# Six fixed PSUM banks in the attention, and one mask-and-maximum step for four of them

## The chip, the core and the metric

The kernel runs on one core of a Trainium2 chip. The metric is the device time of one execution in microseconds (us). A core has engines that run side by side and in order, each from its own instruction queue: TensorE (PE, with its weight loads shown as PEld), VectorE (DVE), ScalarE (ACT), GpSimd (POOL) and SyncE (SP, which issues most DMAs here). They are tied together by semaphores: an instruction may wait until another engine's counter has reached a value. PE writes its results into PSUM, which has eight banks of 512 fp32 columns; DVE and ACT read them from there.

## The reference

One transformer block with a parallel sum: the layer norm of x feeds both an attention with a sliding window and a gated feed-forward part, and both are added to x.

```python
S, D, H, W = 2048, 640, 32, 256; Dh = 20; Df = 1728
xn = layernorm(x)
q, k, v = split(xn @ wqkv)                       # 32 heads of 20 columns
scores = einsum("bhqd,bhkd->bhqk", q, k) * Dh ** -0.5
mask = (idx[:, None] - idx[None, :] >= 0) & (idx[:, None] - idx[None, :] < W)
p = softmax(where(mask, scores, -1e9))
attn = einsum("bhqk,bhkd->bhqd", p, v) @ wo
ffn = (gelu(xn @ w_gate) * (xn @ w_up)) @ w_down
out = x + attn + ffn
```

## The kernel before, in words

The program has four stretches: layer norm and the first projections (to about 107 us), the attention with other matmuls mixed in (to about 570 us), the rest of the feed-forward's gate and up matmuls (to about 804 us), and the output matmuls.

The attention works through 32 units: 8 groups of 4 heads times 4 chunks of 512 queries. A unit u needs three kinds of PE work, all of them written by one hand-made order of slots (`attention()`, line 805; 14 slots per unit, `NS`), which PE, DVE, ACT, POOL and SP follow as written:

- **Maxima.** The softmax's row maxima are computed first, from a bfloat16 product. `max_pair(u, i)` (line 503) fills two banks (`ps_m`) with 128 rows by up to 288 keys, by 16 or more small matmuls (L523) that sit side by side in the array, and DVE then adds the mask and takes the maximum in one instruction per bank (L527), which the profile shows as two rows, CUSTOM_DVE_ANT_0 and DVE_READ_ACCUMULATOR2_ANT. Two pairs make a *burst* of four banks; `BURSTS` puts one at slots 0, 4 and 8, and in slot 0 a second one follows the `av` step below. Twelve slots ahead of unit 0 do seven bursts in advance. A unit has four bursts, which belong to a later unit. After the last one, `max_end` transposes the maxima through PE (`ps_n`, L544), ACT copies them out (`mr`, L546), and a DMA puts them into the rows of q so that the score matmul subtracts them.
- **Scores.** `exp_piece(u, s)` (line 568) fills one bank (`ps_e`, L582, one or two matmuls, 512 columns in all) and ACT takes the exponential into SBUF (`P`, L584). A unit has twelve pieces; `SCORES` says which stand in which slot: 1, 4, 2, 2 and 3 of them in slots 0, 2, 4, 8 and 10. POOL clears the masked corners (L595, L598).
- **The value product.** `av_unit(u - 1)` (line 601) multiplies `P` with v into one bank (`ps_o`, L609) in slot 0, between its two bursts, and ACT copies it out (`ob`, L613).

Between them each slot runs RATE / NS = 2.43 steps of *filler*: dense matmuls of the projections and of the feed-forward part (`ps_d` and `ps_v`, L110), whose two banks come from another pool (`psd`). Small DVE and ACT steps of these projections are put behind the slot's own work by `late` and `flush`.

All the attention's banks come from one pool of six:

```python
psr = pp.enter_context(tc.tile_pool(name="psr", bufs=6, space=PSUM, reuse_waits="tile"))
def bank(name):
    return psr.tile([128, C], F32, name=name, tag="ring")
```

Each call of `bank` gives a new tile in the next of six buffers, and the first instruction that writes it waits for whoever read that buffer's last tile. These waits are put in when the program is built.

Of the kernel before, what the change touches and what calls it, by code (L numbers as in the profile page):

```python
# [9 lines left out]
F32 = mybir.dt.float32  # L10
# [9 lines left out]
C = 512  # L20
# [12 lines left out]
SCORES = {0: range(0, 1), 2: range(1, 5), 4: range(5, 7), 8: range(7, 9), 10: range(9, 12)}  # L33
# [37 lines left out]
def block_kernel(ctx, tc, x, wqk, wv, wgu, wdo, wdl, out):  # L71
# [58 lines left out]
    mask = st1.tile([128, 288], F32, name="mask")  # L130
# [293 lines left out]
    with tc.tile_pool(name="lp", bufs=1, side="right") as lp:  # L424
# [21 lines left out]
        for c in range(1, NC):  # L446
            ln_scale(xs[4 * c:4 * c + 4], lp, mv1 if c == 1 else None)
            vs = [proj_v(v0, 4 * c - 4 + i, None if i % 2 else (psm, "mx")) for i in range(4)]
            if c == 1:
                with tc.manual_schedule(engines={mybir.EngineType.PE}):  # L450
                    lead = (cost for gen in vs for cost in gen)
                    for _ in range(VLEAD):
                        next(lead)
                    ln_turn(4 * c, xs[4 * c:4 * c + 4])
                    run(lead)
            else:
                ln_turn(4 * c, xs[4 * c:4 * c + 4])
            if c + 1 < NC:
                xs += [ln_load(t, lp) for t in range(4 * c + 4, 4 * c + 8)]
            if c == 1:  # L460
                for i in range(NQ):
                    for j in (0, 2):
                        nc.sync.dma_start(qs[i][SR + 2:64, j:j + 2].rearrange("p j t -> p (j t)"), ones[2:4])
            if c == 2:
                for z in range(4):
                    band = mask if z == 0 else lp.tile([128, D], F32, name="xi", tag="xi", bufs=8)[:, 0:288]
                    nc.gpsimd.memset(band, 0.0)
                    nc.gpsimd.affine_select(out=band, in_=band, pattern=[[1, 288]], compare_op=OP.is_ge,
                                            fill=NEG, base=32 * z - 1, channel_multiplier=-1)
                    nc.gpsimd.affine_select(out=band, in_=band, pattern=[[-1, 288]], compare_op=OP.is_ge,  # L470
                                            fill=NEG, base=256 - 32 * z, channel_multiplier=1)
# [26 lines left out]
    def bank(name):  # L498
        return psr.tile([128, C], F32, name=name, tag="ring")

    maxes = {}

    def max_pair(u, i):
        g, c = divmod(u, NC)
        jj, b = divmod(i, 4)
# [3 lines left out]
        n = 128 * b + 128 if c == 0 and b < 2 else 288  # L509
        pss = [bank("ps_m") for _ in range(2)]  # L510
        todo = []
        for h in range(4):
            q0 = 128 * b + 32 * h
            k0 = q0 + 32 - n
            parts = [(max(0, -k0), n, k, max(0, k0), q0 + 32)]
            if k0 < 0:
                parts.append((0, -k0, ks[(u - 1) % NK], C + k0, C) if c else (0, -k0, k, 0, None))
            todo += [(i_, h, q0, *part) for i_, part in enumerate(sorted(parts, key=lambda p: p[1] - p[0]))]
        for _, h, q0, lo, hi, kt, k0, k1 in sorted(todo, key=lambda p: p[:2]):
            for r, ps in enumerate(pss):  # L520
                rows, j = slice(64 * r, 64 * r + SR), 2 * r + jj
                keys = kt[rows, j, k0:k1] if k1 else kt[rows, j, 0:1].to_broadcast([SR, hi])
                nc.tensor.matmul(ps[32 * h:32 * h + 32, lo:hi], q[rows, j, q0:q0 + 32], keys,  # L523
                                 start=True, stop=True, tile_position=(64 * r, 32 * h))
        junk = ap.tile([128, 288], BF, name="junk", tag="junk", bufs=1)
        for r, ps in enumerate(pss):
            nc.vector.tensor_tensor_reduce(out=junk[:, 0:n], in0=ps[:, 0:n], in1=mask[:, 288 - n:288], scale=1.0,  # L527
                                           scalar=NEG, op0=OP.add, op1=OP.max,
                                           accum_out=maxes[u][:, 2 * r + jj, b:b + 1])
# [11 lines left out]
    def max_end(u):  # L541
        nm = maxes.pop(u)
        ps = bank("ps_n")
# [24 lines left out]
    def exp_piece(u, s):  # L568
# [9 lines left out]
        ps = bank("ps_e")  # L578
# [22 lines left out]
    def av_unit(u):  # L601
        g, c = divmod(u, NC)
        o, v = bank("ps_o"), vtiles[g]
# [179 lines left out]
    stream = ((u, i) for u in range(NU) for i in range(8))  # L783
# [3 lines left out]
    def pull_max(n, slot):  # L787
        for _ in range(n):
# [3 lines left out]
            max_pair(*x)  # L792
            if x[1] == 7:
# [11 lines left out]
    def attention():  # L805
# [18 lines left out]
        for u in range(NU + 1):  # L824
            for i in range(NS):
# [9 lines left out]
                for s in SCORES.get(i, ()) if u < NU else ():  # L835
                    exp_piece(u, s)
# [672 lines left out]
```

## Time and profile before

| | before |
|---|---|
| time, median of 3 runs (lowest to highest) | 1046.93 us (1046.66 to 1049.24) |
| the profiled execution: own time, span of its trace | 1046.71 us, 1045.0 us |
| busy: PE, DVE, ACT, POOL | 1034.0, 717.1, 513.6, 335.9 us |
| attention, 107.5 to 553 us of the span: PE, DVE, ACT, POOL busy | 441.90, 271.55, 278.41, 264.72 us of 445.5 |
| maxima on DVE (L527, 512 banks) | 227.9 us, and 42.6 us for the accumulator reads |

A span runs from the first to the last instruction; the profiled execution's own time is 1.7 us more. Busy time counts the time in which at least one instruction of the engine is open; PE's matmuls overlap each other, so a row of PE is longer than the time that it keeps the next one away. "idle before" in a row is the idle time of the engine just ahead of it, with an arrow to the instruction that ended it. The chain of waits follows the work that ended last back from the end: it gives each stretch to the engine that held it.

### The profile page before, as it was taken

How to read it: one execution, taken by the hardware profiler on the slowest of the kernel's cores; microseconds unless marked ns; L12 is line 12 of the kernel's file. 1: busy time of each engine (PE TensorE's matmuls, PEld its weight loads, DVE VectorE, ACT ScalarE, POOL GpSimd, SP SyncE). 2: the span in 40 equal slices, each digit the busy share in tenths (PEclk: the TensorE clock that was granted, in tenths of full speed). 3: DMA queues.
4: the chain of work that ended last, by engine and by line, in shares of the span. 5: the costliest groups of instructions: out<-in, count | busy, mean ns of one | idle time of the engine just before them, and what ended most of it. 6: DMA issues, size and time to landing. Idle time of an engine off the chain costs nothing.

```text
span 1045.0 us, 25814 instructions
## 1 busy us (share of the span) xinstructions
PE 1034.0 (99%) x9533; PEld 826.2 (79%) x9533; DVE 717.1 (69%) x2007; ACT 513.6 (49%) x1088; POOL 335.9 (32%) x511
## 2 busy tenths in 40 slices
PE   8999999999999999999999999999999999999998
PEld 8987666666677766666667888888888999999998
DVE  8745656666655556666663678877656888888887
ACT  4444666765665666555656522223324553333332
POOL 5222767766464458464634111110110000000000
PEclk9999999999999999999999999999999999999999
DMA  5552465545332355444322556677217864443342
GB/s 200 189 150 61 136 185 157 174 152 183 98 117 74 106 148 153 129 131 140 103 80 82 191 193 235 220 254 246 100 61 255 272 232 137 136 128 114 124 136 92
DMA packets 105192, 158.76 MB, mean 152 GB/s; under 512 B 15421, under 2 KB 60093, under 8 KB 105065
## 3 DMA queue, kind: packets, MB, share of 16 engines
q1 hardware_dynamic: 102680, 150.95, 45.1%
q10 hardware_dynamic: 2384, 6.16, 1.8%
q8 instruction: 75, 1.23, 0.5%
q14 instruction: 53, 0.43, 0.1%
HBM read 101.78 MB, written 54.92 MB: 150 GB/s over the span
## 4 chain that ended last, share of the span: by engine, by line
PE 89%; DVE 3%; DMA 3%; POOL 2%; SPq 1%; ACT 1%; issue 1%; DVEq 0%; POOLq 0%
PE ps_g L953 21%; PE ps L1220 21%; PE ps_d L110 19%; PE ps_e L582 7%; PE ps_v L110 7%; PE ps_o L609 7%; PE ps_m L523 4%; PE ps_g L110 1%; DMA qs<-qd 1%; SPq L494 1%; PE ps_t L181 1%; DMA qd<-pt 1%; POOL pt L259 1%; PE ps_d L356 1%; POOL wql L643 0%
## 5 line engine op out<-in xcount | busy, mean ns | idle before, releaser
L527 DVE CUSTOM_DVE_ANT_0 junk<-ps_m,mask 128x288 bf16<-128x288 f32 (+2 forms) x512 | 227.9, 445 | 155.0 <-PE ps_m L523 97.2
L584 ACT ACTIVATE P<-ps_e 128x512 f32<-128x512 f32 (+2 forms) x384 | 195.6, 578 | 59.8 <-PE ps_e L582 56.1
L1220 PE MATMUL ps<-wb,at 128*128 128x320 f32 x999 | 155.9, 309 | 0.0
L1220 PEld LDWEIGHTS ps<-wb,at 128*128 128x128 f32 x999 | 148.9, 188 | 0.2
L595 POOL TENSOR_SCALAR_AFFINE_SELECT P<-P 128x512 f32<-128x512 f32 x128 | 84.6, 663 | 139.1 <-ACT P L584 138.1
L582 PE MATMUL ps_e<-qs,ks 124*128 124x128 bf16 (+2 forms) x704 | 107.4, 277 | 0.6 <-DVE mx L527 0.5
L110 PE MATMUL ps_d<-xh,wqh 128*128 128x512 f32 x350 | 104.3, 410 | 0.0
L110 PE MATMUL ps_d<-xl,wqh 128*128 128x512 f32 x350 | 104.3, 409 | 0.0
L110 PE MATMUL ps_d<-xh,wql 128*128 128x512 f32 x350 | 103.9, 409 | 0.0
L1220 PE MATMUL ps<-wt,at 128*128 128x320 f32 x552 | 89.3, 309 | 0.4 <-DVE u L1058 0.4
L582 PEld LDWEIGHTS <-ks 124*128 124x128 bf16 x704 | 50.9, 98 | 46.5 <-issue 29.0
L609 PE MATMUL ps_o<-P,v 128*32 128x384 f32 (+2 forms) x1408 | 84.9, 386 | 0.7 <-POOL P L598 0.7
L1220 PEld LDWEIGHTS ps<-wt,at 128*128 128x128 f32 x552 | 82.9, 188 | 0.9 <-DVE u L1058 0.9
L598 POOL TENSOR_SCALAR_AFFINE_SELECT P<-P 128x512 f32<-128x512 f32 x112 | 70.3, 638 | 33.6 <-ACT P L584 33.6
L1174 ACT ACTIVATE at<-ss 128x512 fp32r<-128x512 f32 x59 | 37.3, 632 | 87.6 <-DVE ss L1058 87.5
L103 POOL TENSOR_TENSOR wql<-wr,wqh 128x640 fp32r<-128x640 f32 x11 | 17.6, 1607 | 174.8 <-PE ps_g L953 149.5
L609 PEld LDWEIGHTS ps_o<-P,v 128*32 128x32 f32 x1408 | 41.0, 109 | 40.5 <-issue 20.4
L110 PEld LDWEIGHTS ps_d<-xh,wql 128*128 128x128 f32 x350 | 63.9, 189 | 11.1 <-issue 0.4
L110 PEld LDWEIGHTS ps_d<-xl,wqh 128*128 128x128 f32 x350 | 63.8, 189 | 10.4 <-issue 0.2
L110 PEld LDWEIGHTS ps_d<-xh,wqh 128*128 128x128 f32 x350 | 63.5, 189 | 10.7 <-issue 0.2
L259 POOL TENSOR_TENSOR pt<-r,pt 128x512 bf16<-128x512 f32 x40 | 46.8, 1169 | 63.2 <-ACT pt L258 63.0
L613 ACT ACTIVATE ob<-ps_o 128x512 f32<-128x512 f32 x32 | 19.1, 598 | 86.3 <-PE ps_o L609 76.1
(194 smaller groups left out, 1846.8 us busy)
## 6 DMA issues: line engine op xcount, KB each, us to landing
hr<-hd SPq DMA_DIRECT2D x104, 128.0 KB
hd<-he SPq DMA_DIRECT2D x50, 256.0 KB
wr<-wgu SPq DMA_DIRECT2D x27, 320.0 KB
qs<-qd SPq DMA_DIRECT2D x64, 120.0 KB
ks<-kd SPq DMA_DIRECT2D x64, 120.0 KB
xi<-x SPq DMA_DIRECT2D x16, 320.0 KB
qs<-qd SPq DMA_DIRECT2D x64, 80.0 KB
ks<-kd SPq DMA_DIRECT2D x64, 80.0 KB
```

The lines of the kernel that those rows point to most:

```text
L110: nc.tensor.matmul(ps, a(k), b(k), start=n == 0, stop=n == 3 * nk - 1)
L259: nc.gpsimd.tensor_tensor(out=pt[:, l, :], in0=r, in1=pt[:, 1, :], op=OP.subtract)
L523: nc.tensor.matmul(ps[32 * h:32 * h + 32, lo:hi], q[rows, j, q0:q0 + 32], keys, start=True, stop=True, tile_position=(64 * r, 32 * h))
L527: nc.vector.tensor_tensor_reduce(out=junk[:, 0:n], in0=ps[:, 0:n], in1=mask[:, 288 - n:288], scale=1.0, scalar=NEG, op0=OP.add, op1=OP.max ...
L582: nc.tensor.matmul(ps[:, col:col + n], k[0:QROWS, j, kc:kc + 128], q[0:QROWS, j, q0:q0 + n], start=True, stop=True)
L584: nc.scalar.activation(pt[:, j, lo:hi], ps[:, lo:hi], AF.Exp, scale=SCALE)
L595: nc.gpsimd.affine_select(out=a, in_=a, pattern=[[0, 4], [1, 128]], compare_op=OP.is_ge, fill=0.0, base=0, channel_multiplier=-1)
L598: nc.gpsimd.affine_select(out=a, in_=a, pattern=[[0, 4], [-1, 128]], compare_op=OP.is_ge, fill=0.0, base=-1, channel_multiplier=1)
L609: nc.tensor.matmul(o[32 * j:32 * j + 32, q0:q0 + n], v[:, w0_:w0_ + 32], pt[:, j, col:col + n], start=i == 0, stop=i == len(todo) - 1, ski ...
L953: nc.tensor.matmul(ps, i, j, start=first and n == 0, stop=n == len(work) - 1, skip_group_check=True)
L1174: nc.scalar.activation(hi[:, 3:7], s, AF.Copy)
L1220: nc.tensor.matmul(ps[bank][:, 0:HD], *work[bank][j], start=bank not in begun, stop=final[p, bank] == n and j == len(work[bank]) - 1, skip ...
```

## The change

The pool has one tile, `ring`, of six banks, and each use has its bank by number: banks 0 to 3 for the burst, bank 4 for the value product, the transposed maxima and score pieces, bank 5 for score pieces alone, and bank 0 also for the last score piece of slots 2 and 6. `SCORES` now gives piece and bank, with 1, 3, 2, 2, 2 and 2 pieces in slots 0, 2, 4, 6, 8 and 10. `max_burst` writes four banks with the same matmuls in the same order. DVE then adds a mask of 32 columns to the first and last 32 of each bank's 288 columns, in place in PSUM (one TENSOR_TENSOR of 128 x 4 x 2 x 32), and one TENSOR_REDUCE takes the maxima of all four banks (128 x 4 x 288); for the first burst of either half of a unit with c = 0 the two pairs differ in width, so that the mask step has half the columns and there are two reduces. The mask tile shrinks from 288 to 64 columns.

```diff
-SCORES = {0: range(0, 1), 2: range(1, 5), 4: range(5, 7), 8: range(7, 9), 10: range(9, 12)}
+SCORES = {0: ((0, 5),), 2: ((1, 4), (2, 5), (3, 0)), 4: ((4, 4), (5, 5)), 6: ((6, 5), (7, 0)),
+          8: ((8, 4), (9, 5)), 10: ((10, 4), (11, 5))}
...
-    mask = st1.tile([128, 288], F32, name="mask")
+    mask = st1.tile([128, 1, 2, 32], F32, name="mask")
...
-    psr = pp.enter_context(tc.tile_pool(name="psr", bufs=6, space=PSUM, reuse_waits="tile"))
+    psr = pp.enter_context(tc.tile_pool(name="psr", bufs=1, space=PSUM, reuse_waits="tile"))
+    ring = psr.tile([128, 6, C], F32, name="ring")
...
-    def bank(name):
-        return psr.tile([128, C], F32, name=name, tag="ring")
-
     maxes = {}
 
-    def max_pair(u, i):
+    def max_burst(u, i):
...
+        for z in range(2):
+            b = b0 + z
+            n = 128 * b + 128 if c == 0 and b < 2 else 288
...
+                    nc.tensor.matmul(ring[32 * h:32 * h + 32, 2 * z + r, 288 - n + lo:288 - n + hi],
+                                     q[rows, j, q0:q0 + 32], keys, start=True, stop=True,
+                                     tile_position=(64 * r, 32 * h))
+        four = ring[:, 0:4]
+        first = 0 if sizes[0] == 288 else 1
+        edges = four.rearrange("p k (a b) -> p k a b", a=2)[:, :, first:2, 0:32]
+        nc.vector.tensor_tensor(out=edges, in0=edges, in1=mask[:, :, first:2].to_broadcast([128, 4, 2 - first, 32]),
+                                op=OP.add)
+        best = maxes[u].rearrange("p (r j) b -> p j b r", r=2)[:, jj]
+        for z0, z1 in ((0, 2),) if sizes[0] == sizes[1] else ((0, 1), (1, 2)):
+            nc.vector.tensor_reduce(out=best[:, b0 + z0:b0 + z1],
+                                    in_=four[:, 2 * z0:2 * z1, 288 - sizes[z0]:288].rearrange(
+                                        "p (b r) k -> p b r k", r=2), op=OP.max, axis=mybir.AxisListType.X)
...
     def max_end(u):
         nm = maxes.pop(u)
-        ps = bank("ps_n")
+        ps = ring[:, 4]
...
-    def exp_piece(u, s):
+    def exp_piece(u, s, bank):
...
-        ps = bank("ps_e")
+        ps = ring[:, bank]
...
     def av_unit(u):
         g, c = divmod(u, NC)
-        o, v = bank("ps_o"), vtiles[g]
+        o, v = ring[:, 4], vtiles[g]
...
     def pull_max(n, slot):
-        for _ in range(n):
+        for _ in range(n // 2):
...
-            max_pair(*x)
-            if x[1] == 7:
+            max_burst(*x)
+            if x[1] == 6:
```

The instructions of PE stand in nearly the same order as before; what differs are the score pieces' slots and what the instructions wait for. The rows below stand in one unit late in the attention (its score pieces have c = 0, so that each is a single matmul of 384 columns), each with the semaphores that it waits for in brackets: DVE_49, Activation_49, Pool_49 and PE_49 count what these engines have done, DMAHW ones what DMAs have landed. The line numbers of the new program are about ten higher (L523 is L525 there, L582 is L591, L609 is L618, L110 is L111).

**PE, slot 0, from the end of the first burst into the value product.** Before, the last matmuls of the burst and the first of the value product:

```order
L523 MATMUL ps_m<-ks_170,qs_168 32x256
L523 LDWEIGHTS qs_168
L523 MATMUL ps_m<-ks_170,qs_168 32x256
L609 MATMUL ps_o<-P,v 32x384 [waits Activation_49,Pool_49]
L609 MATMUL ps_o<-P,v 32x384 x3
L609 MATMUL ps_o<-P,v 32x128 [waits Pool_49]
L609 MATMUL ps_o<-P,v 32x128 x3
```

and now:

```order
L525 MATMUL ring<-ks_170,qs_168 32x256
L525 LDWEIGHTS qs_168
L525 MATMUL ring<-ks_170,qs_168 32x256
L618 MATMUL ring<-P,v 32x384 [waits DVE_49,Pool_49]
L618 MATMUL ring<-P,v 32x384 x3
L618 MATMUL ring<-P,v 32x128 [waits Pool_49]
L618 MATMUL ring<-P,v 32x128 x3
```

The wait for ACT on the value product's first matmul has become a wait for DVE. By the counts in the two programs it was for an exponential of the unit before, the one that read this buffer last; now it is for the TENSOR_REDUCE of the burst just ahead of it, which reads banks 0 to 3, while the value product goes to bank 4.

**PE, slot 0, the start of the second burst behind the value product.** Before:

```order
L609 MATMUL ps_o<-P,v 32x128 [waits Pool_49]
L609 MATMUL ps_o<-P,v 32x128 x3
L523 LDWEIGHTS qs_168
L523 MATMUL ps_m<-ks_170,qs_168 32x288 [waits PE_49]
L523 LDWEIGHTS qs_168
L523 MATMUL ps_m<-ks_170,qs_168 32x288 [waits DVE_49]
```

and now:

```order
L618 MATMUL ring<-P,v 32x128 [waits Pool_49]
L618 MATMUL ring<-P,v 32x128 x3
L525 LDWEIGHTS qs_168
L525 MATMUL ring<-ks_170,qs_168 32x288 [waits Activation_49]
L525 LDWEIGHTS qs_168
L525 MATMUL ring<-ks_170,qs_168 32x288
```

The first matmul waited for PE, the second for DVE (an accumulator read of the first burst). Now the first waits for ACT: by the counts, for the copy `ob` of the value product that stands just ahead of it.

**PE, from the end of the second burst through the score pieces of slots 0 and 2.** Before:

```order
L523 LDWEIGHTS qs_168
L523 MATMUL ps_m<-ks_170,qs_168 32x288
L582 LDWEIGHTS ks_169 [waits DMAHW3_49]
L582 MATMUL ps_e<-qs_167,ks_169 128x384 [waits DVE_49]
L110 MATMUL ps_d<-xl_83,wqh 128x512 x4
L110 MATMUL ps_d<-xh_79,wqh 128x512
L582 LDWEIGHTS ks_169
L582 MATMUL ps_e<-qs_167,ks_169 128x384 [waits Activation_49]
L582 LDWEIGHTS ks_169
L582 MATMUL ps_e<-qs_167,ks_169 128x384 [waits DVE_49]
L582 LDWEIGHTS ks_169
L582 MATMUL ps_e<-qs_167,ks_169 128x384 [waits Activation_49]
```

and now:

```order
L525 LDWEIGHTS qs_168
L525 MATMUL ring<-ks_170,qs_168 32x288
L591 LDWEIGHTS ks_169 [waits DMAHW5_49]
L591 MATMUL ring<-qs_167,ks_169 128x384 [waits DVE_49]
L111 MATMUL ps_d<-xl_83,wqh 128x512 x4
L111 MATMUL ps_d<-xh_79,wqh 128x512
L591 LDWEIGHTS ks_169
L591 MATMUL ring<-qs_167,ks_169 128x384 [waits Activation_49]
L591 LDWEIGHTS ks_169
L591 MATMUL ring<-qs_167,ks_169 128x384 [waits Activation_49]
L591 LDWEIGHTS ks_169
L591 MATMUL ring<-qs_167,ks_169 128x384 [waits Activation_49]
```

Piece 0 (the first 128x384 row) waits for DVE in both. By the counts it was an accumulator read of the first burst before, and is now the TENSOR_REDUCE of the second burst, just ahead of it. Pieces 1, 2 and 3 waited for `ob`, for an accumulator read of the second burst on DVE and for ACT's exponential of piece 0; now each of them waits for the exponential of the piece just ahead, whatever its bank. The slots 4, 6, 8 and 10 follow the same pattern: what writes `ring` waits for the last instruction that read it, in any bank.

More of the change, by code (lines that the diff above doesn't have):

```diff
@@ L465, in block_kernel @@
                 for z in range(4):
-                    band = mask if z == 0 else lp.tile([128, D], F32, name="xi", tag="xi", bufs=8)[:, 0:288]
+                    band = mask if z == 0 else lp.tile([128, D], F32, name="xi", tag="xi", bufs=8)[:, 0:64].rearrange(
+                        "p (o a b) -> p o a b", o=1, a=2)
                     nc.gpsimd.memset(band, 0.0)
[L468 to L471, printed above, removed]
+                    for a, base, sign in ((0, 32 * z - 1, 1), (1, -32 * z, -1)):
+                        nc.gpsimd.affine_select(out=band[:, 0, a], in_=band[:, 0, a], pattern=[[sign, 32]],
+                                                compare_op=OP.is_ge, fill=NEG, base=base, channel_multiplier=-sign)
                     if z:
@@ L508, in max_pair @@
             maxes[u] = ap.tile([128, 4, 4], F32, name="mx", tag="mx")
[L509 to L525, printed above, removed]
@@ L530, in max_pair @@
+        i += 1
         if i == 7:
@@ L782, in block_kernel @@
     NU = NG * NC
-    stream = ((u, i) for u in range(NU) for i in range(8))
+    stream = ((u, i) for u in range(NU) for i in range(0, 8, 2))
     fill = filler()
@@ L834, in attention @@
                     pull_max(2, T)
-                for s in SCORES.get(i, ()) if u < NU else ():
-                    exp_piece(u, s)
+                for s, bank in SCORES.get(i, ()) if u < NU else ():
+                    exp_piece(u, s, bank)
                 flush()
```

20 lines of the change are left out of this document (15 added, 5 removed).

## The prediction

> **What bounds the kernel now.** First the page's busy times and its clock row, then the attention alone in the view of engine time by windows:
>
> ```profile
> PE 1034.0 (99%) x9533; PEld 826.2 (79%) x9533; DVE 717.1 (69%) x2007; ACT 513.6 (49%) x1088; POOL 335.9 (32%) x511
> PEclk9999999999999999999999999999999999999999
> ...
> 107.50:553.00 445.50, 441.90 (x5808) 295.27 (x5810) 271.55 (x1066) 278.41 (x605) 264.72 (x419) 1.00 0.44 132
> ```
>
> PE is open for 441.9 of the attention's 445.5 us at a clock of 1.00, DVE for 271.6, ACT for 278.4. So the attention lasts as long as its matmuls, and whatever DVE gains there can save at most the 3.6 us in which PE stood idle. A wait that PE does not have yet is paid in full, since PE has no slack. Next I read the chain of waits for one unit (start, length, what):
>
> ```profile
> 494.03 0.29 PE ps_m L523 x15
> 494.32 2.75 PE ps_o L609 x48
> 497.07 0.37 PE ps_m L523 x16
> 497.44 0.32 PE ps_e L582 x2
> 497.76 1.16 PE ps_d L110 x5
> 498.92 0.89 PE ps_e L582 x8
> ...
> 501.34 0.56 PE ps_e L582 x4
> ...
> 506.41 0.67 PE ps_e L582 x6
> ```
>
> It is all PE, back to back: burst, value product, burst, score pieces, filler, and so on. Nothing in it waits for DVE or ACT, because each bank is released alone and the ring is six deep. PE's total of waits for DVE in the score pieces says the same (us in all, times, longest):
>
> ```profile
> PE ps_e L582 <- DVE mx L527: 0.5, 2, 0.3
> ```
>
> **The change part by part.** *Less work on DVE.* A burst now costs four mask-and-maximum steps that start 0.61 us apart (497.38 to 497.99 below), 2.44 us. They become one mask step and one reduce. Rows by form (last figures: busy us, mean ns):
>
> ```profile
> L527 DVE CUSTOM_DVE_ANT_0 junk<-ps_m,mask 128x288 bf16<-128x288 f32 x448 | 205.0, 458 | 135.1 <-PE ps_m L523 84.2 <-DVE mx L527 0.5 <-PE ps_e L582 0.5
> L527 DVE CUSTOM_DVE_ANT_0 junk<-ps_m,mask 128x128 bf16<-128x128 f32 x32 | 9.3, 291 | 15.3 <-PE ps_m L523 13.0
> L1058 DVE TENSOR_TENSOR ss<-hr 128x256 f32<-128x256 f32 x59 | 24.9, 423 | 1.3
> ```
>
> The mask step has 4 x 2 x 32 = 256 columns: 0.42 us by the 128x256 row. No TENSOR_REDUCE stands in the trace. The L527 rows give (458 - 291) / 160 = 1.04 ns per column and 0.16 us fixed, so 1152 columns take 0.16 + 1.20 = 1.36 us. Bounds: 1.20 (no fixed part) and 4 x 0.46 = 1.83 (each bank as a pass of its own); I take 1.36, as one instruction over one strided read is nearest to one long row. With 0.03 us between them (below) that is 1.81 us against 2.44, some 0.6 us per burst and about 80 us of DVE over 128 bursts. It is worth nothing in time: PE bounds. The smaller mask is likewise less work for POOL ahead of the attention, and PE does not wait for it.
>
> *What is released when.* This decides. In the new program `ring` is one tile, and by the waits that the build put in, a write to any of its banks waits for the last instruction that read any of them. PE takes its matmuls in order, so each such wait holds the filler behind it too. Counted through the whole program, these waits stand with no filler ahead of them: 121 straight behind a burst, for that burst's reduce (30 at the value product, 91 at a score piece; the seven bursts in advance have filler behind them); 31 behind a value product, for its copy `ob`; 192 at a score piece, for the exponential of the piece just ahead (two in slot 2, one each in slots 4, 6, 8 and 10, times 32 units); 31 at piece 6, for the copy `mr` of the transposed maxima. The others have two slots of filler or more ahead.
>
> Their price needs the moments at which one engine follows another. From the timeline in one unit, and from the start of the kernel for releases into PE and within DVE:
>
> ```profile
> 497.00 0.44 PE L523 MATMUL ps_m<-ks,qs 60*32 60x288 bf16 x16
> 497.13 0.60 ACT L613 ACTIVATE ob<-ps_o 128x512 f32<-128x512 f32 x1 [3.36 <-PE ps_o L609]
> 497.37 0.39 PE L582 MATMUL ps_e<-qs,ks 124*128 124x128 bf16 x2
> 497.38 0.46 DVE L527 CUSTOM_DVE_ANT_0 junk<-ps_m,mask 128x288 bf16<-128x288 f32 x1 [1.19 <-PE ps_m L523]
> 497.86 0.60 ACT L584 ACTIVATE P<-ps_e 128x512 f32<-128x512 f32 x1
> 497.99 0.46 DVE L527 CUSTOM_DVE_ANT_0 junk<-ps_m,mask 128x288 bf16<-128x288 f32 x1
> ...
> 502.91 0.23 PE L544 MATMUL ps_n<-identb,nm 128*128 128x128 bf16 x1
> 502.94 0.94 PE L110 MATMUL ps_d<-xh,wql 128*128 128x512 f32 x3
> 503.17 0.27 ACT L546 ACTIVATE mr<-ps_n 32x128 bf16<-32x128 f32 x1
> ```
>
> ```profile
> 10.45 0.40 ACT L352 ACTIVATE xh<-ps_t 128x256 fp32r<-128x256 f32 x1
> 10.90 0.39 PE L356 MATMUL ps_d<-xh,wqh 128*128 128x256 f32 x1 [0.69 <-ACT xh L352]
> 11.14 0.16 DVE L158 TENSOR_TENSOR ve<-ve,rs 128x2 f32<-128x2 f32 x1
> 11.33 0.16 DVE L159 SCALAR_TENSOR_TENSOR ve<-ve,rs 128x2 f32<-128x2 f32 x1
> 11.73 1.90 DVE L164 TENSOR_SCALAR xi<-xi,mv,rs 128x640 f32<-128x640 f32 x2
> 13.68 0.55 PE L181 MATMUL ps_t<-ident,xi 128*128 128x128 f32 x3 [0.29 <-DVE xi L164]
> ```
>
> ACT releases PE in 10.90 - 10.85 = 0.05 us, DVE releases PE in 13.68 - 13.63 = 0.05, a DVE step follows the one it needs in 11.33 - 11.30 = 0.03, and an exponential starts 497.86 - 497.76 = 0.10 after its matmuls' end.
>
> - *Behind a burst.* It starts at 497.00 and ends at 497.44; the mask step begins about 0.05 later (an estimate, as `ob` follows the value product by 497.13 - 497.07 = 0.06). Then 0.42 + 0.03 + 1.36 + 0.05: PE goes on at 499.35 instead of 497.37, a stall of **1.98 us**. Fourteen of the 121 are the narrow bursts of c = 0 (128 mask columns, 768 for the reduces), about 0.34 less each. Sum: 121 x 1.98 - 14 x 0.34 = **235 us**.
> - *Behind the value product.* The burst would start at 497.13 + 0.60 + 0.05 = 497.78 instead of 497.00: 0.78 x 31 = **24 us**.
> - *From score piece to score piece.* Matmuls 0.39, 0.10 to the exponential, 0.60, 0.05 back: 1.14 us from piece to piece, where the row of four pieces (0.89) gives 0.22 now. Stall 0.92 x 192 = 177; in the eight units with c = 0 four of the six steps have shorter exponentials,
>
> ```profile
> L584 ACT ACTIVATE P<-ps_e 128x512 f32<-128x512 f32 x320 | 171.9, 605 | 50.0 <-PE ps_e L582 47.3
> L584 ACT ACTIVATE P<-ps_e 128x384 f32<-128x384 f32 x32 | 14.0, 495 | 4.0 <-PE ps_e L582 3.5
> L584 ACT ACTIVATE P<-ps_e 128x256 f32<-128x256 f32 x32 | 11.6, 389 | 5.8 <-PE ps_e L582 5.3
> ```
>
>   2 x 0.11 + 2 x 0.22 = 0.65 less per unit, 5 us in all: **171 us**.
> - *At the maxima's transpose.* Piece 6 follows `mr`: 503.17 + 0.27 + 0.05 = 503.49 instead of 502.94: 0.55 x 31 = **17 us**.
>
> Where filler stands between, the wait is covered: two slots are five steps, 1.16 us in the chain's rows, and with the piece's own 0.22 that is more than the 1.14 of a piece's round trip. That cover fails only where ACT is late. ACT's other work can do that. In 107.5 to 553 us it is 278.4 us less exponentials (197.5), `ob` and `mr` (about 27), some 54 us, and part of it stands in ACT's queue just ahead of a slot's exponentials. Bounds 0 and 54; I take 10, since most of it will run while PE is held by DVE. The slots now hold six groups of score pieces instead of five. The rows 0.32, 0.56, 0.67 and 0.89 for 1, 2, 3 and 4 pieces give about 0.1 us per group beside the pieces, 3 us over 32 units, which the 3.6 us of old idle time cancels.
>
> *The sum*: 235 + 24 + 171 + 17 + 10 = 457 us on the profiled span of 1045.0, which makes 1502; its own time lies 1.7 higher, 1504, and the median of the runs 0.2 above that: **1504 us**, 44% more. A unit would take about 29 us instead of 15.
>
> A row on the clock bears on this, since PE would then be idle for half of the attention in pieces of up to 2 us:
>
> ```profile
> 10.20:13.60 3.40, 1.91 (x13) 1.51 (x12) 3.26 (x10) 2.44 (x8) 3.40 (x11) 1.00 0.81 321
> 1040.00:1045.00 5.00, 1.61 (x12) 1.35 (x10) 1.38 (x3) 0.00 (x0) 0.00 (x0) 0.87 0.27 98
> ```
>
> With PE busy for 1.91 of 3.40 us (longest pause 0.69) the clock stayed at 1.00; after the last matmul it fell. That is the nearest row, and by it I leave the clock alone. The Trainium skill, page TensorE: Matmul & The Clock Gate, Part 1, says that the clock halves after an idle window of about 3.4 us: by that rule no pause here is long enough, and the sum stands. The same page, A second HAM failure mode: psum-queue depth-cycling, reports a kernel whose short idles between groups of matmuls made the clock swing between half and full: by that one the second rival below would come. No run here shows which holds at pauses of 2 us.
>
> **The rivals.**
> *The waits cost nothing.* Place: the first matmul behind a burst. If PE were held only by what its own bank needs, all would be covered. The second burst needs the first one's reduce, 0.05 + 0.42 + 0.03 + 1.36 + 0.05 = 1.91 us after its end, and the value product takes 2.75. Piece 3 in bank 0 needs the second burst's reduce at 499.35, and its turn is about 499.4. The burst of slot 4 needs piece 3's exponential 1.14 us after the piece's start, and has 0.22 + 1.16. Then only the sixth group costs, and the time is 1046 to 1050, say 1048, no change. For it speaks that nothing the arithmetic needs crosses banks; against it that the waits are in the program. It decides from the point where PE's pause at the value product is near 0 instead of 2 us.
> *The clock falls as well.* If PE ran at half clock for half of the attention, its 441.9 us would be worked at 0.75 on average: 441.9 / 0.75 - 441.9 = 147 more, 1651 us. For it: about 1 us of PE work in the 3.4 us around slot 8. Against it: the 56% busy row at 1.00.
>
> **How the numbers follow.** The forecast has 0.80, the falling clock 0.14, the waits that cost nothing 0.05, anything else 0.01. Bounds around 1504: the reduce 121 x -0.16 = -19 or 121 x 0.47 = +57; a tenth of a microsecond on each of the 192 round trips, 19 either way; ACT's other work -10 or +44. All low ends give 1456, all high ends 1624; they will not fall together, and the upper one leans into the clock's case, so I take 1450 to 1600. About 0.78 of the chance lies there. A measurement of this kernel can tell about 0.3% from no change. Slower by more than that: 0.95; within it: 0.04, nearly all of the first rival; faster: 0.01.
>
> **What would show it.** Right: PE busy about as long as before, but some 69% of the span; idle time ahead of PE's L591 and L618 put down to DVE's reduce (L535), near 2.0 us each; L591 put down to ACT's L593, near 0.9 each; L525 behind the value product to L622; the dense stretches after the attention unchanged; the reduce at 1.2 to 1.9 us; DVE somewhat less busy, not more. The second rival shows as a PEclk row below 9 in the attention, the first as PE at 99% still. I am wrong if PE's pauses behind a burst are under 1 us, or if score pieces follow each other by 0.22 us.

## The result: 63% slower, and the profile after

The changed kernel takes 1709.65 us (median of 4 runs, 1705.58 to 1716.91) against 1046.8 us for the one before: a ratio of 1.6347, 95% interval 1.6317 to 1.6377. Forecast were 1504 us, with a range of 1450 to 1600, so the direction was right and the time lies outside the range, above it. The profiled execution has a span of 1704.1 us, 659 us more than before. From the page after, the busy times and the clock row (40 slices of 42.6 us, the granted clock in tenths):

```profile
PE 1288.8 (76%) x9533; PEld 967.2 (57%) x9533; DVE 707.5 (42%) x1255; ACT 544.2 (32%) x1088; POOL 331.6 (19%) x511
PEclk9976775776776778787667767876999999999999
```

The same 9533 matmuls are open for 1289 us instead of 1034, while the clock row, all nines before, lies between 5 and 8 throughout the attention. DVE has about 10 us less work than before. PE's waits (us in all, times, longest):

```profile
PE ring L591 <- DVE mx L535: 181.0, 91, 2.4
PE ring L591 <- ACT P L593: 131.7, 192, 1.0
PE ring L618 <- DVE mx L535: 51.2, 26, 2.1
PE ring L525 <- ACT ob L622: 21.0, 30, 0.7
PE ring L591 <- ACT mr L555: 11.1, 31, 0.4
```

They stand at the places that the prediction counted: 91 score pieces and (with four that the view puts down to POOL and that are as long, 2.1 us) 30 value products behind a burst's reduce, 192 pieces behind the exponential of the one ahead, 31 behind `mr`, 30 bursts behind `ob`. In the timeline (start, length, and in brackets the idle time ahead and what ended it) slot 8 of one unit now reads:

```profile
801.10 0.68 PE L525 MATMUL ring<-ks,qs 60*32 60x288 bf16 x16
801.91 0.43 DVE L531 TENSOR_TENSOR ring<-ring,mask 128x256 f32<-128x256 f32 x1 [4.86 <-PE ring L525]
802.38 1.36 DVE L535 TENSOR_REDUCE mx<-ring 128x4 f32<-128x1152 f32 x1
803.79 0.38 PE L591 MATMUL ring<-qs,ks 124*128 124x128 bf16 x2 [2.01 <-DVE mx L535]
804.26 0.60 ACT L593 ACTIVATE P<-ring 128x512 f32<-128x512 f32 x1 [4.16 <-PE ring L591]
804.90 0.38 PE L591 MATMUL ring<-qs,ks 124*128 124x128 bf16 x2 [0.73 <-ACT P L593]
```

The burst ends, PE stands still for 2.01 us while DVE reads four banks that the next matmul does not touch, then again for 0.73 us behind an exponential. What the prediction left out of its sum is in the view by windows (us of the window; then PE, PEld, DVE, ACT and POOL busy; the granted clock, DMA share, GB/s):

```profile
300.00:500.00 200.00, 128.68 (x1110) 78.22 (x1094) 48.13 (x71) 57.38 (x104) 59.32 (x88) 0.74 0.24 70
900.00:1100.00 200.00, 127.08 (x1065) 77.01 (x1064) 53.13 (x77) 56.91 (x103) 45.70 (x74) 0.75 0.16 49
107.00:1225.00 1118.00, 717.71 (x6051) 449.62 (x6054) 269.48 (x389) 324.04 (x635) 275.23 (x436) 0.74 0.18 54
1220.00:1400.00 180.00, 179.12 (x827) 146.58 (x826) 130.20 (x218) 61.55 (x113) 22.27 (x17) 1.00 0.61 208
```

The attention (third row) takes 1118 us at a mean clock of 0.74. In the dense stretch behind it (last row) the clock is 1.00 again. The filler's rows show it too, 556 ns where it was 410:

```profile
L111 PE MATMUL ps_d<-xh,wqh 128*128 128x512 f32 x350 | 150.7, 556 | 0.0
```

### The profile page after: what moved, and what is told of

It is laid out like the page before. It is cut to its first block, busy times and chain, and to the rows that moved or that the text cites. A ratio compares the mean times of both kernels' runs of the same rounds, so it can differ in the third digit from the quotient of the medians.

```text
span 1704.1 us, 24729 instructions
## 1 busy us (share of the span) xinstructions
PE 1288.8 (76%) x9533; PEld 967.2 (57%) x9533; DVE 707.5 (42%) x1255; ACT 544.2 (32%) x1088; POOL 331.6 (19%) x511
## 4 chain that ended last, share of the span: by engine, by line
PE 71%; DVE 13%; ACT 9%; issue 4%; POOL 1%; DMA 1%; ACTq 0%; DVEq 0%; SPq 0%; POOLq 0%
PE ps_d L111 19%; PE ps_g L962 13%; PE ps L1229 13%; PE ring L591 9%; DVE mx L535 9%; ACT P L593 6%; PE ring L618 6%; PE ps_v L111 5%; PE ring L525 4%; DVE ring L531 3%; ACT ob L622 1%; PE ps_g L111 1%; ACT mr L555 0%; PE ps_t L182 0%; PE ps_d L357 0%
## 5 line engine op out<-in xcount | busy, mean ns | idle before, releaser
L591 PE MATMUL ring<-qs,ks 124*128 124x128 bf16 (+2 forms) x704 | 181.2, 341 | 324.6 <-DVE mx L535 181.0
L593 ACT ACTIVATE P<-ring 128x512 f32<-128x512 f32 (+2 forms) x384 | 219.3, 571 | 500.9 <-PE ring L591 493.5
L531 DVE TENSOR_TENSOR ring<-ring,mask 128x256 f32<-128x256 f32 (+1 forms) x128 | 53.2, 416 | 642.9 <-PE ring L525 626.7
L591 PEld LDWEIGHTS <-ks 124*128 124x128 bf16 x704 | 67.6, 114 | 400.9 <-issue 395.6
L535 DVE TENSOR_REDUCE mx<-ring 128x4 f32<-128x1152 f32 (+1 forms) x144 | 168.6, 1180 | 4.4
L618 PE MATMUL ring<-P,v 128*32 128x384 f32 (+2 forms) x1408 | 113.1, 482 | 59.6 <-DVE mx L535 51.2
L111 PE MATMUL ps_d<-xh,wqh 128*128 128x512 f32 x350 | 150.7, 556 | 0.0
L111 PE MATMUL ps_d<-xh,wql 128*128 128x512 f32 x350 | 148.6, 549 | 0.0
L111 PE MATMUL ps_d<-xl,wqh 128*128 128x512 f32 x350 | 147.7, 546 | 0.0
L618 PEld LDWEIGHTS ring<-P,v 128*32 128x32 f32 x1408 | 61.3, 131 | 107.5 <-issue 74.5
L111 PEld LDWEIGHTS ps_d<-xl,wqh 128*128 128x128 f32 x350 | 88.5, 259 | 31.6 <-issue 14.7
L111 PEld LDWEIGHTS ps_d<-xh,wqh 128*128 128x128 f32 x350 | 91.0, 267 | 23.5 <-issue 6.0
L111 PEld LDWEIGHTS ps_d<-xh,wql 128*128 128x128 f32 x350 | 89.7, 262 | 24.8 <-issue 7.2
L525 PE MATMUL ring<-ks,qs 60*32 60x288 bf16 (+5 forms) x3008 | 65.1, 276 | 21.7 <-ACT ob L622 21.0
```

Of the source, the lines that this page charges most:

```text
L111: nc.tensor.matmul(ps, a(k), b(k), start=n == 0, stop=n == 3 * nk - 1)
L525: nc.tensor.matmul(ring[32 * h:32 * h + 32, 2 * z + r, 288 - n + lo:288 - n + hi], q[rows, j, q0:q0 + 32], keys, start=True, stop=True, ti ...
L531: nc.vector.tensor_tensor(out=edges, in0=edges, in1=mask[:, :, first:2].to_broadcast([128, 4, 2 - first, 32]), op=OP.add)
L535: nc.vector.tensor_reduce(out=best[:, b0 + z0:b0 + z1], in_=four[:, 2 * z0:2 * z1, 288 - sizes[z0]:288].rearrange("p (b r) k -> p b r k", ...
L591: nc.tensor.matmul(ps[:, col:col + n], k[0:QROWS, j, kc:kc + 128], q[0:QROWS, j, q0:q0 + n], start=True, stop=True)
L593: nc.scalar.activation(pt[:, j, lo:hi], ps[:, lo:hi], AF.Exp, scale=SCALE)
```

## The experiments

All were timed beside runs of the kernel before on the same chip (1045.5 to 1046.4 us there), runs 2, 4, 5 and 6 once each, the others 4 to 11 times. The theory after the result: `ring` as one tile makes PE wait for readers of other banks (about 440 us), and the pauses pull the clock down (about 220 us). Its rivals: DVE's new instructions are at fault, the banks' fixed numbers are, or the new slots are.

**1. The same DVE work, fewer banks in the tile.** Banks 4 and 5 become tiles of their own; banks 0 to 3, the burst's, stay one:

```diff
-    ring = psr.tile([128, 6, C], F32, name="ring")
+    ring = psr.tile([128, 4, C], F32, name="ring")
+    own = [psr.tile([128, C], F32, name=f"own{i}") for i in (4, 5)]
+    def bank_of(n):
+        return ring[:, n] if n < 4 else own[n - 4]
```

> Edit: banks 0 to 3 stay one tile of four banks, banks 4 and 5 become tiles of their own; the order of the work, the DVE step and the bank of every piece are those of the change. In the built program the 121 waits for a reduce straight behind a burst become 91 that PE's own data needs (61 at a piece in bank 0, 30 at the second burst of slot 0), none of the score pieces waits for the piece just ahead of it, and no burst waits for ob. Theory 'tile' (the change's time comes from waits across banks of one tile, and the clock fell because of them): 1046 to 1055 us, PE back at 98% or more, clock 1.00. Rival 'DVE step' (the merged step that reads and writes four banks in place is what holds PE): over 1250 us, with PE idle ahead of the second burst and the pieces in bank 0.

Measured: 1064.9 us, ratio 1.0173 (1.0151 to 1.0195). Of the 663 us, 645 are gone with this edit, at the same instructions, the same slots and the same bank numbers. PE is busy for 98% again (the page), and nearly all waits have vanished (PE's largest below, in the same columns as above):

```profile
PE 1043.2 (98%) x9533; PEld 829.6 (78%) x9533; DVE 709.5 (67%) x1255; ACT 515.8 (49%) x1088; POOL 331.5 (31%) x511
```

```profile
PE ring L596 <- DVE mx L540: 4.9, 17, 0.5
```

So what holds PE is the extent of the tile. The time is 10 us above what was expected, though; runs 7 to 10 look for that.

**2. One tile, the old DVE steps.** All six banks in one tile, but the four old mask-and-maximum instructions per burst and the old mask:

```diff
-        nc.vector.tensor_tensor(out=edges, in0=edges, in1=mask..., op=OP.add)
-            nc.vector.tensor_reduce(out=best..., in_=four..., op=OP.max, ...)
+                nc.vector.tensor_tensor_reduce(out=junk[:, 0:n], in0=ring[:, 2 * z + r, 288 - n:288], in1=mask..., ...)
```

> Edit: the change's one tile, bank numbers and slots, but with the old DVE step, four mask-and-maximum instructions per burst and the mask of 288 columns. Theory 'tile': the pause behind a burst is 4 x 0.61 = 2.4 us and more instead of 2.0, 121 times, so some 57 us longer than the change and a little more time at half clock: 1740 to 1830 us, clock 0.80 to 0.83. Rival 'DVE step': 1046 to 1100 us, since the merged step is gone.

Measured: 1738.36 us at a clock of 0.819. Waits of PE:

```profile
PE ring L587 <- DVE mx L531: 197.9, 91, 2.6
PE ring L614 <- DVE mx L531: 60.8, 28, 2.4
```

The loss comes without the new instructions as well, and is 29 us larger, since PE then waits 2.17 us behind a burst (197.9 / 91) instead of 1.99 (181.0 / 91). The pause was expected at 2.4 us, so the time lies 2 us below its range of 1740 to 1830. Merging the mask steps makes DVE's part shorter, as forecast; the rival that blames it falls.

**3. Is it the clock? Zero matmuls in the pauses.** If the clock costs some 200 us, more work in the pauses must make the kernel faster. 1756 matmuls with weights of zero, accumulated into the filler's open banks (they add nothing to any result), stand behind the bursts, value products and transposes and behind six of a unit's twelve score pieces, wherever such a bank is open:

```diff
+                nc.tensor.matmul(ps, zeros, fives[:, 0:cols], start=False, stop=False, ...)
```

> Edit: the change as it is, with 1756 extra matmuls of zero weights that add zero to the open bank of the dense matmuls, put where PE pauses: about 1.75 us of them behind each burst, 0.65 behind the value product and between score pieces, 0.43 behind the transpose. They leave the results and the waits as they are. Theory 'clock' (the pauses themselves cost about 445 us, the rest of the change's 660 us is matmuls at half clock, and the clock falls only because PE does too little): clock 0.97 or more in the attention, and 1480 to 1540 us, so the kernel is faster by 170 to 230 us with more work. Rival 'waits alone' (the waits cost all of it, by releases that are slower than I took): 1700 us or more, since the pauses stay as they are or grow.

Measured: 1509.17 us, ratio 1.4419 (1.4381 to 1.4456): 200 us less than the change, with 18% more matmuls. The clock is 0.995. The forecast of 1504, which had left the clock alone, is 5 us away. From the page:

```profile
PE 1433.4 (95%) x11289; PEld 1000.6 (67%) x11289; DVE 705.8 (47%) x1255; ACT 542.7 (36%) x1088; POOL 332.1 (22%) x513
PEclk9999999999999999999999999999999999999999
```

The waits of PE that are left where most of them were:

```profile
PE ring L610 <- DVE mx L552: 25.2, 75, 2.0
PE ring L610 <- ACT P L614: 13.2, 29, 1.1
```

This is not a pure measure of the waits. Where the zero matmuls outlast a pause they add time of their own (only 29 of 192 exponentials are still waited for), so the 200 us are the least that the clock costs, and that the time comes within 5 us of 1504 is in part luck.

**4. What the zero matmuls cost where there are no pauses.** The same 1756 in the split of run 1.

> Edit: the split tiles of the first experiment, with the same 1756 zero matmuls as in the padded kernel, where PE has no pauses to hide them. Theory: they cost their length, 1756 times 0.135 to 0.22 us, some 300 to 370 us: 1360 to 1440 us at clock 1.00. That prices the work that the padded kernel took on while it got faster by 200 us. Rival 'zero matmuls cost PE next to nothing' (then their help in the padded kernel says little on filled pauses): under 1150 us.

Measured: 1396.05 us, 331 us above the split, 0.19 us each. So they are not free; in the one-tile kernel they ran in time that PE had lost.

**5. Half of the waits: two tiles, of four banks and of two.** The burst no longer holds pieces in banks 4 and 5, but those two banks still hold each other:

```diff
+    ring = psr.tile([128, 4, C], F32, name="ring")
+    two = psr.tile([128, 2, C], F32, name="two")
```

> Edit: banks 0 to 3 one tile, banks 4 and 5 together a second tile of two. The waits behind a burst are gone; left are 128 waits from score piece to score piece, 31 of piece 6 for mr, 31 of piece 0 for ob. Theory 'each wait is paid, and the clock falls only where PE is busy for less than about 0.4 of 3.4 us': 128 x 0.92 - 3 = 115, mr 17, ob 31 x 0.41 = 13, in all 145 us, so 1180 to 1210 us at a clock of 0.98 or more. Rival 'any short pauses make the clock swing': the same 145 us and a clock under 0.93, 1240 us or more.

Measured: 1187.03 us at a clock of 0.999. Waits of PE:

```profile
PE two L596 <- ACT P L598: 93.6, 128, 1.8
PE two L596 <- ACT mr L560: 11.9, 31, 0.6
PE two L596 <- ACT ob L627: 9.7, 27, 0.7
```

The 128 steps between banks 4 and 5 (of 192) wait and the others do not. Pauses of about 0.7 us alone leave the clock up.

**6. Long pauses, but less often: banks 0 to 4 in one tile, bank 5 apart.**

```diff
+    ring = psr.tile([128, 5, C], F32, name="ring")
+    own5 = psr.tile([128, C], F32, name="own5")
```

> Edit: one tile of five banks (0 to 4) and bank 5 as a tile of its own. Left are 30 waits of the value product and 60 of pieces 4 and 8 for the reduce straight behind a burst (2 us each, as in the change), 30 of the second burst for ob, 31 of piece 7 for mr, 32 of piece 3 for the exponential of piece 1, and piece 1 some 0.4 us short of the second burst's reduce. So pauses as long as the change's, but with more work around each. Theory 'busy share' (the clock falls where PE is busy for less than about 0.4 of 3.4 us, whatever the single pause): 178 + 23 + 10 + 13 + 21 = 245 us of pauses, PE busy for at least 0.42 around each, so a clock of 0.94 or more and 1290 to 1345 us. Rival 'pause length' (a pause of 2 us brings half clock by itself): the clock near the change's 0.83, at most 0.88, and 1380 us or more.

Measured: 1339.08 us, clock 0.972. The waits behind bursts stand at as many places as in the change. Those of the value product are as long (2.0 us on average), but those of the score pieces average 1.52 us (138.4 / 91) instead of 1.99: in the trace 60 of the 91 are 1.6 us or longer, and the other 31 are 0.5 to 0.8 us:

```profile
PE ring L596 <- DVE mx L540: 138.4, 91, 2.8
PE ring L623 <- DVE mx L540: 49.7, 25, 2.1
```

So some 90 long pauses are left of the change's 121, and the clock fell 21 times instead of 91. A pause of about 2 us does not bring the clock down by itself; what differs is how much PE works around it.

**7. Where do the split's 18 us come from? Pairs.** Two tiles of two banks each, a mask step and a reduce for each pair, and piece 7 in bank 2:

```diff
+    ring = [psr.tile([128, 2, C], F32, name=f"ring{z}") for z in range(2)]
```

> Edit: banks 0 and 1, 2 and 3 as two tiles of two banks, banks 4 and 5 tiles of their own; mask step and reduce once per pair instead of once per burst, and piece 7 in bank 2 instead of bank 0. Theory 'bank 0 late' (what is left in the split kernel, 17 us over the kernel before, is piece 3 behind the four-bank reduce and the burst of slot 8 behind piece 7's exponential in bank 0): a pair's steps end about 1.1 us after its matmuls instead of 1.9, so 1046 to 1056 us. Rival 'the slots' (the sixth group of score pieces and their new places cost it): 1060 us or more, as in the split kernel.

Measured: 1065.3 us, ratio 1.0179 (1.0165 to 1.0193): no gain. The run does not decide, since the waits that it was to shorten did not go: pieces wait for a reduce for 7.3 us in 22 waits, where it was 4.9 us, of the 18, in 17 waits in run 1. The number is that of the rival, the slots, but the next run takes its reason away.

**8. The new slots alone.** The kernel before with the pieces in the new slots, and nothing else:

```diff
-SCORES = {0: range(0, 1), 2: range(1, 5), 4: range(5, 7), 8: range(7, 9), 10: range(9, 12)}
+SCORES = {0: range(0, 1), 2: range(1, 4), 4: range(4, 6), 6: range(6, 8), 8: range(8, 10), 10: range(10, 12)}
```

> Question: what does the new table of slots cost by itself? The kernel before, with its six banks in rotation and its old mask step, but with the score pieces in slots 0, 2, 4, 6, 8 and 10 as in the change. Theory 'the slots': most of what the split still lacks lies in the sixth group and in the order of the pieces, about 0.35 us per unit, so 1053 to 1058 us. Rival 'the fixed banks': what is left comes from banks that are released later when their numbers are fixed and four are taken at once; then the slots alone cost no more than the prediction's 0.1 us per group, 3 us over 32 units, and the time is 1046 to 1050 us.

Measured: 1044.04 us, ratio 0.9980 (0.9971 to 0.9989). The first theory falls, and the rival is right in kind: the slots cost nothing, they even gain 2 us. It is the only part of the change that helps, and this kernel is the fastest of all here, by 0.2%: less than the prediction counts as a change, though the interval stays below 1.

**9. Fixed numbers, each bank its own tile, old DVE steps.** The kernel of run 2 with six tiles:

```diff
-    ring = psr.tile([128, 6, C], F32, name="ring")
+    ring = [psr.tile([128, C], F32, name=f"ring{i}") for i in range(6)]
```

> Question: are fixed banks as good as a rotation when each is a tile? Six tiles of one bank each, with the change's bank numbers and slots, and the old four steps on VectorE with the old mask (the one-tile form of the same took 1738 us). Theory 'the tile': everything large comes from one tile over six banks; with six tiles nothing is held across banks, and the time is that of the new slots alone within 3 us, 1050 to 1060 us. Rival 'the fixed numbers': pieces 3 and 7 in bank 0 and the transposed maxima in bank 4 wait for the last user of that very bank; then it is 5 us or more above the kernel that has only the new slots.

Measured: 1054.29 us, ratio 1.0076 (1.0064 to 1.0089), 684 us below run 2. It is 10 us above run 8, so the rival's mark (5 us or more) is reached: fixed numbers cost something against a rotation. Part of it is seen as bursts that wait for an exponential in one of their own banks, for instance

```profile
495.03 0.44 PE L525 MATMUL ring<-ks,qs 60*32 60x288 bf16 x16 [0.26 <-ACT P L589]
```

From 107.5 to 570 us PE is idle for 6.3 us in this kernel and for 3.0 in run 8; the other 7 us do not appear as idle time, and their cause stays open.

**10. The mask's building.** Run 1 with the mask in 288 columns again, of which DVE's mask step reads the first and the last 32:

```diff
-    mask = st1.tile([128, 1, 2, 32], F32, name="mask")
+    ends = st1.tile([128, 1, 9, 32], F32, name="mask")
+    mask = ends.rearrange("p o a b -> p (o a b)")
```

> Question: does the new building of the mask lose 4 us before the attention, and why? One 4-bank tile and banks 4 and 5 as tiles of their own, as in the split (1064.9 us), but the mask is built again in 288 columns, by two selections that stand apart in POOL's order. Theory 'POOL holds VectorE': in every kernel with the small mask, POOL runs two short selections and then three multiplications of 128x320 without a pause, and VectorE's two scalings of xi (L165) take 4.15 us instead of 1.90 meanwhile, which delays TensorE's third transposes by 2.4 us. With the old mask they take 1.9 us again, the first burst of the attention comes 3.5 to 4 us earlier, and the time is 1060.5 to 1061.5 us. Rival 'the pools': the shift comes from the attention's tiles or from when inputs land; then L165 keeps its 4.1 us and the time stays within 1064 to 1066.

Measured: 1059.44 us, ratio 1.0131 (1.0117 to 1.0144); by the spans, 1057.5 against 1061.3, 3.8 us less than run 1. The median lies 1 us below the expected range. The expected place is right. In the change, DVE's two scalings of xi take 4.15 us while POOL works through three multiplications in a row, and PE waits for the second of them:

```profile
11.89 4.15 DVE L165 TENSOR_SCALAR xi<-xi,mv,rs 128x640 f32<-128x640 f32 x2
...
12.62 0.61 POOL L471 TENSOR_SCALAR_AFFINE_SELECT mask<-mask 128x32 f32<-128x32 f32 x2
...
13.05 0.33 PE L182 MATMUL ps_t<-ident,xi 128*128 128x128 f32 x1 [0.42 <-DVE xi L165]
13.21 2.48 POOL L303 TENSOR_TENSOR wvl<-wvall,wvh 128x320 fp32r<-128x320 f32 x3
...
16.10 1.41 PE L182 MATMUL ps_t<-ident,xi 128*128 128x128 f32 x9 [2.72 <-DVE xi L165]
```

With the old mask the scalings take 1.90 us (run 10):

```profile
11.60 1.90 DVE L166 TENSOR_SCALAR xi<-xi,mv,rs 128x640 f32<-128x640 f32 x2
...
13.13 1.09 POOL L304 TENSOR_TENSOR wvl<-wvall,wvh 128x320 fp32r<-128x320 f32 x1
...
13.56 1.21 PE L183 MATMUL ps_t<-ident,xi 128*128 128x128 f32 x9 [0.30 <-DVE xi L166]
...
14.18 0.42 POOL L472 TENSOR_SCALAR_AFFINE_SELECT mask<-mask 128x288 f32<-128x288 f32 x1
...
14.58 1.71 POOL L304 TENSOR_TENSOR wvl<-wvall,wvh 128x320 fp32r<-128x320 f32 x2
```

A selection now stands between the multiplications, but it is not what lets the scalings in, as was expected: they are over at 13.50 us, before it begins at 14.18. This time it is POOL's first multiplication that takes longer, 1.09 us against 0.83 (2.48 / 3). Why DVE goes first here and POOL in the change stays open.

The Trainium skill, page SBUF — State Buffer, section Who interferes with whom, says that a VectorE instruction in a two-port mode and GpSimd take a shared pair of ports in turn, and that the one that comes second is blocked for the whole of the other's instruction. The 4.15 us fit that in part only: the second scaling lasted until all three multiplications had ended (13.21 + 2.48 = 15.69 us), not one. That the ports are the cause is the page's word, as the runs show only that the building of the mask decides.

The pause of 2.72 us also costs more than itself. In the change it leaves PE open for 0.85 of 3.41 us, and the next such stretch runs at half clock (columns as in the windows above):

```profile
13.54:16.95 3.41, 0.85 (x8) 0.85 (x9) 3.41 (x4) 0.49 (x2) 2.99 (x5) 1.00 0.07 25
16.95:20.36 3.41, 3.41 (x19) 3.41 (x18) 3.38 (x11) 1.00 (x4) 2.52 (x3) 0.50 0.41 106
```

Run 1 has the same half-clock stretch (16.47 to 19.88 us), run 10 has none. Where the scalings begin the change is 0.29 us behind run 10 (11.89 against 11.60), at the transposes 2.54 (16.10 against 13.56), and after that stretch 4.07 (21.05 against 16.98 at the same matmuls). So the 4 us are a wait and a stretch at half clock.

Put in a row, each as its ratio to the kernel before:

| kernel | ratio | step |
|---|---|---|
| before | 1 | |
| new slots (run 8) | 0.9980 | -2 us |
| and six fixed banks, six tiles (run 9) | 1.0076 | +10 us |
| and four banks as one tile, merged mask step and reduce (run 10) | 1.0131 | +6 us |
| and the small mask (run 1) | 1.0173 | +4 us |
| and all six banks as one tile (the change) | 1.6347 | +645 us |

## Why the prediction was off

**Right: the new steps on DVE, and that they save no time.** The reduce was sized from the old rows at 1.36 us and the mask step at 0.42; they measured 1.36 and 0.43, and a burst occupies DVE for 1.83 us (801.91 to 803.74) where it was 2.44. DVE's busy time fell by only 10 us, though, and not by 80, since most of what was saved had been gaps between the old instructions.

**Right: the waits, in number and size.** The terms beside what the trace after shows, in us:

| term | predicted | measured |
|---|---|---|
| behind a burst | 235 | 181.0 + 51.2 + 8.4 put down to POOL = 241 |
| from piece to piece | 171 | 131.7 idle + 192 x 0.17 = 164 |
| behind the value product | 24 | 21 |
| at `mr` | 17 | 11 idle; the rest can lie under open matmuls |
| ACT's other work | 10 | no wait for ACT beyond those counted |

The 0.17 is the part of the stall in which the two matmuls of a piece stay open (0.39 in the timeline) beyond the 0.22 that a piece costs. The first four together are about 440 us against 447. The forecast's time is about that of the kernel with its clock held up: 1504 predicted, 1509.17 in run 3. The first rival, waits that cost nothing, fell with the 2.01 us pause at L591.

**Wrong: "by it I leave the clock alone".** This is the step that failed: the sum has no term for the clock. 1704 - 1045 - 440 leaves some 220 us, and run 3 gives 200 back by work in the pauses. The row chosen (10.20 to 13.60 us, PE open for 56%, longest pause 0.69 us) was the nearest in the old trace, but the change makes windows with far less work than that. The prediction had the figure that mattered, about 1 us of PE work in the 3.4 us around slot 8, and put it behind that row. Six neighbouring stretches of the changed kernel, cut where the clock changes (columns as in the windows above):

```profile
798.60:802.02 3.42, 2.90 (x22) 1.57 (x22) 0.10 (x1) 0.83 (x2) 1.23 (x2) 0.50 0.26 74
802.02:805.43 3.41, 0.90 (x6) 0.63 (x6) 1.69 (x2) 0.71 (x2) 0.00 (x0) 1.00 0.00 0
805.43:808.84 3.41, 2.72 (x10) 1.64 (x9) 0.00 (x0) 1.60 (x3) 1.16 (x1) 0.50 0.06 16
808.84:812.26 3.42, 3.42 (x10) 2.64 (x9) 0.69 (x1) 2.34 (x4) 2.51 (x4) 0.50 0.78 227
812.26:815.67 3.41, 1.35 (x43) 0.65 (x45) 1.79 (x2) 0.00 (x0) 3.25 (x6) 1.00 0.46 133
815.67:819.08 3.41, 3.41 (x40) 2.05 (x36) 0.00 (x0) 0.00 (x0) 1.70 (x4) 0.50 0.02 5
```

Behind a stretch in which PE was open for 0.90 of 3.41 us (26%), and behind one with 1.35 (40%), the clock is 0.50. It stays there through a stretch with 2.72 open (80%) and is back only after one with 3.42 (100%). The Trainium skill, page TensorE: Matmul & The Clock Gate, Part 1, asks for an idle window of about 3.4 us before the clock halves; the trace differs, since in the window at 802.02 PE works for a quarter of the time and the longest pause is 2.01 us, and the clock falls all the same. The same page's section A second HAM failure mode: psum-queue depth-cycling, which the prediction weighed as a rival, tells of short idles between groups of matmuls that make the clock swing between half and full, which is what these rows show.

**The rival had the mechanism and too low a price.** "The clock falls as well" had 0.14 and 1651 us. Its mean clock of 0.75 came out at 0.74, although half of the time at half clock was assumed there and not worked out; its 147 us were too few, because it spread PE's work evenly over the time. The windows at full clock are those with the pauses, and the work falls into the windows behind them: by the clock's record of the attention 481 us of PE's open time lie in half-clock windows and 237 in full ones. Half of 481 is 240 us lost by open time (some of it is waiting that no clock shortens), 200 to 220 by the two differences above. With that weight its price is 200 to 240 us and its time 1704 to 1744.

**Wrong, and small: "PE does not wait for it".** The smaller mask is less work for POOL, but building it changes what POOL does beside DVE's scalings. PE waits 2.4 us longer for these and then works through a stretch at half clock, and the attention's first value product comes at 108.42 us in run 1 against 104.47 in run 10. **Half right: the slots.** The sixth group was to cost 3 us and cancel against old idle time; it gained 2. **Left out:** the 10 us of fixed numbers and the 6 of the merged tile, which the forecast's 457 us hid.

## What to carry to other kernels

What a wait covers is set, in this build, by the extent of the tile and not of the data (the pool is made with `reuse_waits="tile"`, and no run made it otherwise): before several banks are joined for one wide instruction, list who else writes any part of that tile and price the round trip for each, and give those others tiles of their own (1064.9 instead of 1709.65 us here). When stalls are added to an engine whose clock depends on its load, look at the busy share of each short window and not at the mean or at the longest pause, and put the half clock on the work that follows the gaps. A rotation of banks is worth keeping where PE has no slack: fixed numbers cost 10 us here with every bank its own tile.

## What the runs showed of the hardware

The granted clock in these traces is 1.0 or 0.5, never between, and changes only at steps of 3.413 us; 0.74 is a mixture. Counted over all such steps of the changed kernel's trace, the clock fell 91 times, behind windows in which PE was open for 16 to 46% of the time (half of them under 32%); it stayed up 230 times, behind 39 to 100%. It came back 91 times, behind windows with 79 to 100%, and stayed down 83 times, behind 39 to 83%. So it falls below some 40 to 45% and returns only at about 80%; run 2 has the same bounds (45 and 79%). With banks 0 to 4 in one tile (run 6) it fell 21 times, with the zero matmuls 4 times. That the share of open matmuls is what the hardware counts is an inference; no run varied it by itself. Work done may be the better measure: in the changed kernel's trace the filler's matmuls of 128x512 follow each other by 0.23 us at full clock and by 0.43 at half (medians), so 79 to 83% of a half-clock window is about as much work as 42 to 44% of one at full clock, and one bound could stand behind both. This is an estimate that no run tests.

One reduce over four PSUM banks (1152 columns) took 1.36 us and one over two (576 columns, run 7) 0.76. The 576 columns between them cost 0.60 us, 1.04 ns each, which is what a column cost within one bank before, by the rows of another instruction: crossing from bank to bank in a strided read cost nothing that can be seen.
